# Letting expert 1's weight loads go out while the last attention pairs are still being transposed by DMA

## The chip, the cores and the metric

The kernel runs on one core of one Trainium2 chip. The metric is the device time of one execution in microseconds (us), and a version is judged by the median over several executions.

## The reference

The work is a sparse attention followed by a mixture of eight experts with balanced (Sinkhorn) gates. Shapes: q, k and v are 4 x 8 x 768 x 64 (batch, head, position, feature); the attention output becomes x of 3072 x 512.

```python
k_sum = k.reshape(B, H, nb, 32, D).max(axis=3)      # 24 blocks of 32 keys
v_sum = v.reshape(B, H, nb, 32, D).mean(axis=3)
a = softmax over [ scores within |i-j| < 16 , scores with k_sum + log(32) ]
x = concat heads of ( a @ [v, v_sum] )               # 3072 x 512
P = exp(x @ w_gate - max)
for _ in range(8):
    P /= P.sum(1, keepdims=True); P /= P.sum(0, keepdims=True); P *= N / E
out = sum over e of  P[:, e] * ( relu(x @ w1[e]) @ w2[e] )
```

## The kernel before

Heads are handled in 16 pairs, four for each of the four batch entries. Each pair needs q and k with the features on the partitions (qT, kT), v as it comes (v_x), the two edge strips of v that reach into the neighbouring tile (V_e), scores, exponentials, masks, the values product, a normalisation, and a transposition of the result into xT, the input of the experts. While the pairs run, TensorE also computes expert 0 in plain form (hps, yps). Experts 1 to 7 follow in a long stage with a Strassen-like scheme of seven products per block (pa, pb, pg, xy), which fills the time from about 128 us to the end. Between the two lies the bridge: the eight Sinkhorn rounds on the gates P_sb, spread between the last matmuls of expert 0 and the first of expert 1.

How transfers are issued in the attention part:

- GpSimd (POOL) issues every load from memory: k, q and v of each pair with a cast from 32 to 16 bits, and the expert weights `w1` and `w2`. These go through the software queue q0.
- SyncE (SP) issues, through the hardware queue q1, four small copies for V_e per pair (`near_values`, L362 and L364), for pairs 12 to 15 the transposes of k and q (`tr_dma`, L310), and for pairs 10 to 14 the transpose of the normalised result into xT (`x_dma`, L314). Earlier pairs are transposed by TensorE.
- Each of the two queues has eight completion semaphores that it uses in turn, so that a transfer is issued only when the one eight places earlier in the same queue has landed.

The order of instructions on each engine is fixed when the program is built, by a list scheduler (`Plan`). Each unit of work is entered by `add` with an engine, a planned cost, its dependences, a priority and a `lag`, the planned time after its end until its result can be used. For a DMA the cost is the issue time on the queue and the lag is the planned landing. The plan sets the order alone; the waits at run time are for the real landings.

The loads of expert 1's first weights are entered last of all on POOL: four tiles of `w1` (`load_w1(1, i)`, two DMAs of 128 KB each, L176) and one tile of `w2` (`load_w2(1)`, one DMA of 1024 KB, L187). In front of them stands a unit `hold`. It copies one element of each of the four qT buffers that pairs 12 to 15 use (L820), and so cannot end before the transposes of q of pairs 12 to 15 have landed; POOL runs in order, so the weight loads stand behind it.

Names used later: `kT12`, `qT12`, `near12`, `x10` and so on mean the DMA of that kind for that pair. `logits(b)` (L531) multiplies xT of the four pairs of batch entry b with the gate weights. `normalize` (L509, L510) writes a buffer `xs`, of which there are two; `x_dma` reads it, so the normalisation of pair i+2 cannot write before `x_dma(i)` has landed.

Of the kernel before, what the change touches and what calls it, by code (L numbers as in the profile page):

```python
# [10 lines left out]
BF16 = mybir.dt.bfloat16  # L11
# [22 lines left out]
class Plan:  # L34
# [12 lines left out]
    def add(self, eng, cost, fn, deps=(), prio=0.0, opens=(), uses=(), lag=0.0):  # L47
        u = Unit(eng, cost, fn, [d for d in deps if d is not None], prio, list(opens), lag)
        for b in list(opens) + list(uses):
            b.users.append(u)  # L50
        if uses and eng != "PE":
            u.prio -= 100.0
        self.waiting.append(u)
        return u
# [62 lines left out]
def kernel(  # L117
# [10 lines left out]
    nc = tc.nc  # L128

    B, H, S, D = q.shape  # L130
    G = S // 128
# [6 lines left out]
    NP = (B * H) // 2  # L138
    PB = H // 2
    SCALE = 1.0 / float(D) ** 0.5  # L140
    W = 16
# [4 lines left out]
    VD = D + 1  # L146
# [68 lines left out]
    NB = PB  # L215
    NE = 2
# [7 lines left out]
    attn = early.enter_context(tc.tile_pool(name="attn", bufs=1))  # L224
    aps = early.enter_context(tc.tile_pool(name="aps", bufs=1, space=PSUM))
    if True:

        ident = attn.tile([128, 128], BF16, name="ident")
        held = attn.tile([1, 1], BF16, name="held")
        band = attn.tile([128, LIVE], BF16, name="band")  # L230
        m_blk = attn.tile([128, G, 64], BF16, name="m_blk")
        qT = [attn.tile([128, W + S + W], BF16, name=f"qT{i}") for i in range(NB)]
        kT = [attn.tile([128, S], BF16, name=f"kT{i}") for i in range(NB)]
# [10 lines left out]
        add = plan.add  # L244
# [51 lines left out]
        def tr(i, z, tag):  # L296
            st = at.pop(("st", i, z))
            t = at["t", i, z] = bank(tag, "tkq", BF16)
            for g in range(G):
                if i < PB:  # L300
                    for j in range(2):
                        nc.tensor.transpose(t[64 * j:64 * j + 64, g * 128:(g + 1) * 128],
                                            st[:, j, g, :], ident)
                else:
                    nc.tensor.transpose(t[:, g * 128:(g + 1) * 128],  # L305
                                        st[:, g, :, :].rearrange("p j d -> p (j d)"), ident)

        def tr_dma(i, z):
            r, st = i % NB, at.pop(("st", i, z))
            nc.sync.dma_start_transpose(out=(kT[r][:], qT[r][:, W:W + S])[z].rearrange("c (g t) -> c g t", g=G),  # L310
                                        in_=st[:].rearrange("p g j d -> p (g j d)"))
# [45 lines left out]
        def near_values(i):  # L357

            sv, ve = v_x[i % NQ], V_e[i % NE]
            for j in range(2):  # L360
                c0, q0 = VD * j, 64 + 32 * j
                nc.sync.dma_start(out=ve[q0 + W:q0 + 2 * W, 1:G, c0:c0 + VD],  # L362
                                  in_=sv[128 - W:128, j, 0:G - 1, :])
                nc.sync.dma_start(out=ve[q0:q0 + W, 0:G - 1, c0:c0 + VD],  # L364
                                  in_=sv[0:W, j, 1:G, :])

        def scores(i, h):
            sg = at["sg", i, h] = banks2("sg")
            for s in range(HG):
                for j in range(2):  # L370
                    score_mm(i, sg[:, j, s * LIVE:(s + 1) * LIVE], j, HG * h + s, 0, LIVE)
# [244 lines left out]
        U = {}  # L616
        last = [None, None]
# [19 lines left out]
        def pair_start(i, prio):  # L637
            o = i - NB
            war_k = [U.get(("S", o, 0)), U.get(("S", o, 1)), U.get(("km", o))]
            war_q = war_k[:2] + [U.get(("ss", o, 0)), U.get(("ss", o, 1))]  # L640
            tag = "m" if i < PB else "a"
            for z in range(2 if i >= PB else 1):
                if i >= 12:
                    U["tr", i, z] = U["kT", i, z] = add("SP", 1.25, lambda z=z: tr_dma(i, z),
                                                        [U["kq"[z], i]] + (war_k, war_q)[z], prio, lag=5.0)
                    continue
                buf = Buffer(tag)
                U["tr", i, z] = add("PE", 0.4, lambda z=z: tr(i, z, tag),
                                    [U["kq"[z], i], U["ident"]] + (war_k, war_q)[z]
                                    + [U["tr", i, 0] if z else U.get(("S", i - 1, 1 if i > PB else 0))],  # L650
                                    prio, opens=[buf])
                U["kT", i, z] = add({"ACT": 0.8} if z == 0 else {"ACT": 0.8, "DVE": 0.95},
                                    0, lambda z=z: tr_out(U["kT", i, z].on, i, z), [U["tr", i, z]], prio,
                                    uses=[buf])
            if i < PB:
                query_half(i, 0, prio)
            U["km", i] = add("DVE", 0.95, lambda: key_max(i), [U["kT", i, 0]] + war_q[2:], prio)
            buf = Buffer("a")
            U["vs", i] = add("PE", 0.4, lambda: block_sums(i),
                             [U["v", i]] + ([U.get(("A", i - NE, 1))] if i >= PB else []), prio + 0.01, opens=[buf])  # L660
            U["Vs", i] = add("DVE", 0.36 if i < PB else 0.84, lambda: block_out(i), [U["vs", i]],
                             prio + 0.01, uses=[buf])
# [37 lines left out]
            return U.get((what, n % PB, n // PB)) if n >= 0 else None  # L700

        def pair_whole(i, prio):
            U["near", i] = add("SP", 2.5, lambda: near_values(i), [U["v", i], U.get(("A", i - NE, 1))], prio,
                               lag=1.9)
            for h in range(2):
                buf = Buffer("s")
                U["S", i, h] = add("PE", 0.28, lambda h=h: scores(i, h),
                                   [U["kT", i, 0], U["kT", i, 1], U.get(("ed", i - 2))], prio, opens=[buf])
                U["X", i, h] = add("ACT", 0.97, lambda h=h: score_exp(i, h), [U["S", i, h]], prio, uses=[buf])
                U["mk", i, h] = add("DVE", 0.56, lambda h=h: masks(i, h),  # L710
                                    [U["X", i, h], U.get(("A", i - 2, 1))], prio)
            U["ed", i] = add("DVE", 0.78, lambda: edges(i),
                             [U["X", i, 0], U["X", i, 1], U["mk", i, 1], U.get(("A", i - NE, 1))], prio)
            bufs = [Buffer("a"), Buffer("a")]
            U["ss", i, 0] = U["ss", i, 1] = add("PE", 0.22, lambda: summaries2(i),
                                                [U["km", i], U["kT", i, 1], U.get(("A", i - NE, 1))], prio,
                                                opens=bufs)
            for h in range(2):
                U["sx", i, h] = add("ACT", 0.46, lambda h=h: summary_exp(i, h), [U["ss", i, h]], prio,
                                    uses=[bufs[h]])  # L720
            for h in range(2):
                buf = Buffer("a")
                U["A", i, h] = add("PE", 0.4, lambda h=h: values(i, h),
                                   [U["mk", i, h], U["ed", i], U["sx", i, h], U["Vs", i], U["near", i]],
                                   prio, opens=[buf])
                U["no", i, h] = add("DVE", 0.68, lambda h=h: normalize(i, h),
                                    [U["A", i, h], U.get(("xt", i - 2))], prio, uses=[buf])
            if 10 <= i < 15:
                U["xt", i] = U["x", i] = add("SP", 1.25, lambda: x_dma(i), [U["no", i, 0], U["no", i, 1]], prio,
                                             lag=4.5)  # L730
            else:
                buf = Buffer("a")
                U["xt", i] = add("PE", 0.35, lambda: to_xT(i), [U["no", i, 0], U["no", i, 1]], prio, opens=[buf])
                U["x", i] = add({"ACT": 0.8, "DVE": 0.9}, 0, lambda: x_out(U["x", i].on, i), [U["xt", i]], prio,
                                uses=[buf])
# [55 lines left out]
        c0 = add("DVE", 3.8, constants, [], -5.0)  # L791
# [11 lines left out]
        for i in range(PB, NP):  # L803
# [3 lines left out]
            if i % PB == PB - 1:  # L807
# [7 lines left out]
                    zero.extend(U["w2d"])  # L815
                expert0(b * S, xs)
                expert0(b * S + HS, xs)
        def hold():
            for r in range(12 % NB, NB):
                nc.gpsimd.tensor_copy(out=held[0:1, 0:1], in_=qT[r][0:1, W:W + 1])  # L820

        last[0] = add("POOL", 0.3, hold, [last[0]] + [U["kT", i, 1] for i in range(12, NP)])
        for i in range(4):
            load(("w1n", i), lambda i=i: load_w1(1, i), 0.85, 1.3)
        load("w2n", lambda: load_w2(1), 0.85, 5.0)
# [13 lines left out]
    if True:  # L839
# [351 lines left out]
        for n in range(LAG, len(groups)):  # L1191
            g0, q0 = g, q
            g = group(*groups[n])
            q = pair(*groups[n - LAG])
            e, j, i = groups[n]
# [48 lines left out]
        last = [pair(*groups[len(groups) - LAG + n], spare=bool(n % 2), c1_at=c1s[n], tail=True) for n in range(LAG)]  # L1244
# [6 lines left out]
        A, B, C, D = last  # L1251
# [42 lines left out]
```

## Time and profile before

| what | us |
|---|---|
| median of 7 executions | 676.3 |
| lowest and highest of the 7 | 674.63 and 678.41 |
| the profiled execution | 674.77 |
| span of the profiled execution, first to last instruction | 673.0 |
| TensorE busy in the span | 662.7 |

The profiled execution lies near the low end of the runs; 1.8 us of it lie outside the span. Times below are counted from the start of the span. A timeline row gives start, duration, engine, line, operation and tiles, the number of instructions merged, and in brackets the idle time before it with the one that ended it. A row of the table by stretches gives the stretch and its length, the busy time (and instruction count) of PE, PEld, DVE, ACT and POOL, the granted clock, the summed share of the DMA engines' time taken by packets, and GB/s.

### The profile page before, as it was taken

The numbers are of one execution on the slowest core, as the hardware profiler recorded it, in microseconds if no ns is written. First come the engines' busy times: TensorE is split into PE (matmuls) and PEld (weight loads), VectorE is DVE, ScalarE is ACT, GpSimd is POOL, SyncE is SP. The second block draws the span as 40 slices with busy tenths as digits, with TensorE's granted clock in tenths as the row PEclk, the third lists the DMA queues.
The fourth block names the chain that finished last, engine by engine and source line by source line (L and its number), as shares of the span: only waits on it lengthen the run. The fifth ranks groups of instructions, "written<-read, shape, count | busy, mean of one in ns | idle before, by whom it ended". The sixth has DMA issues, their size and how long they took to land.

```text
span 673.0 us, 13531 instructions
## 1 busy us (share of the span) xinstructions
PE 662.7 (98%) x5111; PEld 434.4 (65%) x5111; DVE 579.7 (86%) x1433; ACT 402.3 (60%) x783; POOL 131.6 (20%) x177
## 2 busy tenths in 40 slices
PE   7999999999999999999999999999999999999996
PEld 4666655555666666666666666666666666666665
DVE  6878889777799988998899988998899889998885
ACT  4777776565777765555655565555555555556552
POOL 8699622122101010201010010101020101100001
PEclk9999999999999999999999999999999999999999
DMA  9999969000613050311422061405031142201224
GB/s 118 190 145 145 151 91 157 10 1 1 79 12 36 1 79 1 37 13 22 58 23 27 1 78 10 39 1 79 1 33 17 22 58 21 29 0 48 82 91 158
DMA packets 124018, 36.46 MB, mean 54 GB/s; under 512 B 110384, under 2 KB 121136, under 8 KB 123952
## 3 DMA queue, kind: packets, MB, share of 16 engines
q0 software_dynamic: 104672, 26.22, 42.2%
q1 hardware_dynamic: 18464, 8.83, 5.9%
q8 instruction: 40, 0.66, 0.4%
q10 hardware_dynamic: 816, 0.54, 0.3%
q14 instruction: 26, 0.21, 0.1%
HBM read 52.45 MB, written 6.29 MB: 87 GB/s over the span
## 4 chain that ended last, share of the span: by engine, by line
PE 93%; DVE 4%; DMA 1%; issue 1%; ACT 0%; POOL 0%; DVEq 0%; ACTq 0%
PE xy L913 36%; PE pg L907 16%; PE pa L907 11%; PE pb L907 11%; PE hps L200 6%; PE yps L210 6%; PE sg L334 1%; DVE hf L857 1%; DMA vx<-in_v_dram 1%; PE vs L342 1%; PE tkq L305 1%; PE av L406 1%; PE av L412 1%; PE ss L430 1%; PE tx L517 0%
## 5 line engine op out<-in xcount | busy, mean ns | idle before, releaser
L913 PEld LDWEIGHTS <-hf 128*128 128x128 f16 x2352 | 230.1, 98 | 95.6 <-issue 0.5
L913 PE MATMUL xy<-w,hf 128*128 128x256 f16 x1312 | 183.4, 273 | 0.0
L913 PE MATMUL xy<-ws,hf 128*128 128x256 f16 x984 | 147.6, 273 | 0.1
L191 ACT ACTIVATE hf<-pg 128x512 f16<-128x512 f32 x84 | 50.2, 597 | 150.9 <-PE pg L907 150.9
L1049 DVE SCALAR_TENSOR_TENSOR out_acc<-xy,P_sb,out_acc 128x512 f32<-128x512 f32 x164 | 115.0, 742 | 2.1 <-PE xy L913 2.1
L854 DVE TENSOR_TENSOR hf<-hf 128x512 f16<-128x512 f16 x252 | 100.0, 423 | 8.8
L907 PE MATMUL pa<-xT,w 128*128 128x512 f16 x336 | 99.9, 379 | 0.0
L907 PEld LDWEIGHTS <-w 128*128 128x128 f16 x672 | 65.8, 98 | 44.3 <-issue 1.1
L857 DVE TENSOR_TENSOR hf<-pb,c 128x512 f16<-128x512 f32 x84 | 58.1, 691 | 38.6 <-PE pb L907 32.4
L176 POOL DMA_DIRECT2D w<-in_moe_w_dram x56 | 41.8, 758 | 220.6 <-PE pg L907 191.9
L907 PEld LDWEIGHTS <-ws 128*128 128x128 f16 x504 | 49.3, 98 | 25.4
L941 ACT COPY c<-pg 128x512 f32<-128x512 f32 x84 | 49.2, 585 | 22.4 <-PE pg L907 22.4
L857 DVE TENSOR_TENSOR hf<-pg,c 128x512 f16<-128x512 f32 x84 | 57.1, 679 | 0.8 <-PE pg L907 0.8
L926 ACT COPY pg<-pa 128x512 f32<-128x512 f32 x84 | 47.9, 570 | 4.8
L191 ACT ACTIVATE hf<-pa 128x512 f16<-128x512 f32 x84 | 50.6, 603 | 0.0
L907 PE MATMUL pg<-xTs,w 128*128 128x512 f16 x168 | 50.0, 379 | 0.2
L907 PE MATMUL pg<-xT,w 128*128 128x512 f16 x168 | 50.0, 379 | 0.1
L907 PE MATMUL pb<-xT,ws 128*128 128x512 f16 x168 | 50.0, 379 | 0.0
L907 PE MATMUL pg<-xTs,ws 128*128 128x512 f16 x168 | 50.0, 379 | 0.0
L907 PE MATMUL pb<-xTs,ws 128*128 128x512 f16 x168 | 50.0, 379 | 0.0
L934 ACT COPY c<-pb 128x512 f32<-128x512 f32 x84 | 49.8, 593 | 0.0
L200 PE MATMUL hps<-xT,w 128*128 128x384 f16 x256 | 48.6, 326 | 0.0
(141 smaller groups left out, 818.1 us busy)
## 6 DMA issues: line engine op xcount, KB each, us to landing
w<-in_moe_w_dram POOLq DMA_DIRECT2D x8, 1024.0 KB, 8.9
w<-in_moe_w_dram POOLq DMA_DIRECT2D x56, 128.0 KB, 3.5
out_dram<-out_acc SPq DMA_DIRECT2D x20, 256.0 KB, 2.0
qst<-in_q_dram POOLq DMA_DIRECT2D x32, 96.0 KB, 5.9
vx<-in_v_dram POOLq DMA_DIRECT2D x16, 192.0 KB, 6.3
kst<-in_k_dram POOLq DMA_DIRECT2D x24, 96.0 KB, 6.3
w<-in_moe_w_dram POOLq DMA_DIRECT2D x2, 512.0 KB, 8.1
kst<-in_k_dram POOLq DMA_DIRECT2D x4, 192.0 KB, 4.7
```

Source lines behind the costliest of these rows:

```text
L176: nc.gpsimd.dma_start(out=t[:, :, h, :], in_=moe_w1[e].rearrange("(dk p) f -> p dk f", p=128)[:, :, f:f + 128])
L191: nc.scalar.activation(out=out, in_=in_, func=AF.Relu, bias=0.0, scale=1.0)
L200: nc.tensor.matmul(hp[:, 0:n], lhsT=w1s[e][:, dk, 128 * f:128 * (f + 1)], rhs=xT[:, dk, t0:t0 + n], start=(dk == 0), stop=(dk == KD - 1))
L210: nc.tensor.matmul(yp[:], lhsT=h[:, f, c * 128:(c + 1) * 128], rhs=w2s[e][:, f, :], start=(f == 0), stop=(f == KF - 1))
L854: nc.vector.tensor_tensor(out=out, in0=in0, in1=in1, op=ALU.subtract)
L857: nc.vector.tensor_tensor(out=out, in0=in0, in1=in1, op=ALU.add)
L907: nc.tensor.matmul(bank[:], lhsT=w[:, dk, :], rhs=x[:, dk, :], start=start and dk == 0, stop=dk == KH - 1, skip_group_check=True)
L913: nc.tensor.matmul(bank, lhsT=a(f)[:, 128 * c:128 * (c + 1)], rhs=w[:, f, :], start=start and f == 0, stop=f == FH - 1, skip_group_check=True)
L926: nc.scalar.copy(out=B["g"][:], in_=B["a"][:])
L934: nc.scalar.copy(out=B["c5"][:], in_=B["b"][:])
L941: nc.scalar.copy(out=B["c2"][:], in_=B["g"][:])
L1049: nc.vector.scalar_tensor_tensor(out=acc, in0=src, scalar=P_sb[:, t, e:e + 1], in1=acc, op0=ALU.mult, op1=ALU.add)
```

## The change

The unit `hold` and its one-element tile are taken out. Three planned lags are set higher. `near_values` gets a choice of issuing engine, which for pair numbers 0 to 15 always gives SyncE as before, since the other branch begins at 16.

```diff
-        held = attn.tile([1, 1], BF16, name="held")
...
-                nc.sync.dma_start(out=ve[q0 + W:q0 + 2 * W, 1:G, c0:c0 + VD],
+                eng = nc.gpsimd if i >= 16 else nc.sync
+                eng.dma_start(out=ve[q0 + W:q0 + 2 * W, 1:G, c0:c0 + VD],
...
                     U["tr", i, z] = U["kT", i, z] = add("SP", 1.25, lambda z=z: tr_dma(i, z),
-                                                        [U["kq"[z], i]] + (war_k, war_q)[z], prio, lag=5.0)
+                                                        [U["kq"[z], i]] + (war_k, war_q)[z], prio, lag=6)
...
-            U["near", i] = add("SP", 2.5, lambda: near_values(i), [U["v", i], U.get(("A", i - NE, 1))], prio,
-                               lag=1.9)
+            U["near", i] = add(*(("POOL", 3.6) if i >= 16 else ("SP", 2.5)), lambda: near_values(i),
+                               [U["v", i], U.get(("A", i - NE, 1))], prio, lag=2.2)
...
                 U["xt", i] = U["x", i] = add("SP", 1.25, lambda: x_dma(i), [U["no", i, 0], U["no", i, 1]], prio,
-                                             lag=4.5)
+                                             lag=5)
...
-        def hold():
-            for r in range(12 % NB, NB):
-                nc.gpsimd.tensor_copy(out=held[0:1, 0:1], in_=qT[r][0:1, W:W + 1])
-
-        last[0] = add("POOL", 0.3, hold, [last[0]] + [U["kT", i, 1] for i in range(12, NP)])
         for i in range(4):
             load(("w1n", i), lambda i=i: load_w1(1, i), 0.85, 1.3)
         load("w2n", lambda: load_w2(1), 0.85, 5.0)
```

In the built program the instructions of TensorE, VectorE, ScalarE and SyncE stand in the same order as before. GpSimd's are the same too but for the four one-element copies, which are gone.

More of the change, by code (lines that the diff above doesn't have):

```diff
@@ L361, in near_values @@
                 c0, q0 = VD * j, 64 + 32 * j
-                nc.sync.dma_start(out=ve[q0 + W:q0 + 2 * W, 1:G, c0:c0 + VD],
+                eng = nc.gpsimd if i >= 16 else nc.sync
+                eng.dma_start(out=ve[q0 + W:q0 + 2 * W, 1:G, c0:c0 + VD],
                                   in_=sv[128 - W:128, j, 0:G - 1, :])
-                nc.sync.dma_start(out=ve[q0:q0 + W, 0:G - 1, c0:c0 + VD],
+                eng.dma_start(out=ve[q0:q0 + W, 0:G - 1, c0:c0 + VD],
                                   in_=sv[0:W, j, 1:G, :])
```

## The prediction

> **What bounds the kernel now.** I read the page's busy times and its chain of waits first, then a table by stretches, then the timelines of POOL, SP and PE around the change.
>
> ```profile
> PE 662.7 (98%) x5111; PEld 434.4 (65%) x5111; DVE 579.7 (86%) x1433; ACT 402.3 (60%) x783; POOL 131.6 (20%) x177
> ...
> PE 93%; DVE 4%; DMA 1%; issue 1%; ACT 0%; POOL 0%; DVEq 0%; ACTq 0%
> ```
>
> TensorE is busy 662.7 of 673.0 us and carries 93% of the chain. The change takes no TensorE work out, so it can act on the time only through TensorE's idle time. The stretches show where that is (first PE, then PEld, DVE, ACT, POOL):
>
> ```profile
> 80.00:98.00 18.00, 18.00 (x183) 10.05 (x181) 15.46 (x40) 14.02 (x22) 1.94 (x6) 1.00 0.87 115
> 98.00:119.00 21.00, 21.00 (x219) 12.05 (x218) 18.69 (x53) 12.23 (x22) 6.68 (x9) 1.00 1.35 144
> 119.00:124.00 5.00, 5.00 (x53) 2.94 (x52) 1.62 (x7) 3.14 (x6) 0.06 (x1) 1.00 0.00 2
> 124.00:155.00 31.00, 30.08 (x161) 15.67 (x160) 26.43 (x70) 17.91 (x36) 6.47 (x11) 1.00 0.00 1
> ```
>
> From 80 to 124 us TensorE has no idle time at all. From 124 to 155 it has 0.9 us, of which 0.8 is a Sinkhorn matmul waiting for DVE. So there is next to nothing to gain in this profile, and every wait that the change adds is paid in full. POOL around the change:
>
> ```profile
> 79.62 1.02 POOL L274 DMA_DIRECT2D vx<-in_v_dram  x1 [2.23 <-PE av L412]
> ...
> 97.41 0.18 POOL L820 COPY held<-qT 1x1 bf16<-1x1 bf16 x1 [6.97 <-DMA qT<-qst]
> 97.86 5.94 POOL L176 DMA_DIRECT2D w<-in_moe_w_dram  x8 [0.28 <-issue]
> 103.73 0.96 POOL L187 DMA_DIRECT2D w<-in_moe_w_dram  x1
> ```
>
> POOL has nothing else to do from 80.6 us on; hold keeps the weights back until 97.9. And the first users of these weights:
>
> ```profile
> 123.11 0.35 DVE L1104 TENSOR_REDUCE rs_sb<-P_sb 128x24 f32<-128x192 f32 x1 [3.27 <-ACT P_sb L535]
> ...
> 123.71 0.23 DVE L857 TENSOR_TENSOR ws<-w 128x256 f16<-128x256 f16 x1
> ```
>
> The last load (w2) lands 14.2 us after its issue, at 117.9. DVE's weight sums stand behind the first Sinkhorn row sum, which waits until 123.1 for the last gate logits and not for weights. Earlier weights start nothing earlier.
>
> **What the skill says.** The Trainium skill, page "DMA: Bandwidth & Descriptors", three places. "Issuing engines are not separate DMA queues": DMAs started by different engines run on the same 16 DMA engines and interleave. "Queues, rings and completion order": a DMA engine takes turns between its queues packet by packet, and a completion count lands only after all earlier writes of that engine, across its queues; so a transpose's landing can be held by another queue's bytes. The trace agrees: transposes that had the engines to themselves (kT14, qT14, x10) landed 2.8 us after issue, those beside the weight loads (x11, x12, x13) 5.7, 9.2 and 10.0 us after. "Rules for kernel authors": a transpose beside ordinary DMAs needs no ordering, so hold is not there for safety; the trace, where x11 to x13 overlap the loads, agrees.
>
> **The change, part by part.**
>
> *Four copies on POOL gone*: 3 x 0.18 + 0.63 = 1.2 us, on an engine that was waiting. Worth 0. *Lags and the engine choice*: instruction order is as before on every engine but POOL; worth 0. *Weight loads earlier*: the eight w1 DMAs are issued from 80.6 us at 0.74 us each (5.94 / 8). Eight completion semaphores rotate: the eighth waits for the landing of v of pair 15 (79.62 + 6.5 = 86.1), and w2 waits for the first w1 DMA. So w2 goes out near 87 to 89 instead of 103.7, all some 15 to 17 us earlier. Gain on the path: 0, by the paragraph above. Their bytes now compete with what SP issues between 80 and 103 us. For each of those transfers: issue from SP's timeline, landing by its own time to landing, and the instruction that waits for its semaphore:
>
> | transfer | issued | landed | first wait | slack |
> |---|---|---|---|---|
> | near11 | 80.75 to 82.67 | 86.8 | PE 93.1 | 6.3 |
> | qT13 | 83.44 | 87.0 | PE 93.7 | 6.7 |
> | kT14, qT14 | 85.53, 86.90 | 88.3, 89.7 | PE 101.0 | 11.3 |
> | near12 | 88.22 to 90.13 | 92.1 | PE 100.4 | 8.3 |
> | x10 | 90.83 | 93.6 | DVE 100.75 (buffer xs) | 7.1 |
> | kT15, qT15 | 92.24, 93.62 | 96.7, 97.3 | PE 105.6 | 8.3 |
> | near13 | 94.93 to 97.36 | 99.3 | PE 105.0 | 5.7 |
> | x11 | 98.46 | 104.2 | PE 104.25 | 0.05 |
> | x12 | 103.71 | 112.9 | DVE 113.4 (buffer xs) | 0.5 |
> | x13 | 108.38 | 118.36 | DVE 118.38 (buffer xs) | 0.0 |
>
> The key row is x11. logits of batch entry 2 (L531, 24 small matmuls) need it:
>
> ```profile
> 98.46 1.78 SPq L314 DMA_TRANSPOSE xT<-xs  x1
> ...
> 103.98 0.87 PEld L531 LDWEIGHTS <-xT 128*128 128x128 f16 x24
> ```
>
> Before, x11 went out just behind the first w1 load and landed with 0.05 us to spare. After, it goes out behind nearly all the weights.
>
> *When will x11 land?* I count DMA work. A transpose: kT14 and qT14 landed 1.35 us apart with SP issuing that far apart (upper end); 192 KB at the 215 GB/s of that stretch is 0.9 (lower end); I take 1.1. A near set: 0.4, an estimate from its 41 KB. The weights: in the stage before, the engines were busy from about 99 to 118.4, 19.4 us, with x11, x12, x13 and two near sets in it: 19.4 - 3.3 - 0.8 = 15.3 us for 2 MB, losses from mixing included; at the 155 to 175 GB/s of that stage the bytes alone take about 12.6. So 12.6 to 15.3. Where does this fit in? The DMA shares between 85 and 97 us add up to 5.8 busy of 12 us:
>
> ```profile
> DMA  1899319990599502020202049960899349980092
> ```
>
> so 6.2 us are free there, and about 1.7 more from 97 to 99: 7.9 in all. At 99 us there are then 12.6 - 7.9 = 4.7 to 15.3 - 7.9 = 7.4 us of work still queued when x11 enters. If x11 waits for all of it, it lands at 99 + 4.7 + 1.1 + 0.3 = 105.1 to 107.8 (0.3 from last byte to landing, what is left of 2.8 us). The nearest rows, x12 and x13, which also entered behind w2, took 9.2 and 10.0 us: 107.7 to 108.5. I take 106.8, so TensorE waits 106.8 - 104.2 = 2.6 us at L531. Bounds: 0 if x11 takes its turns without its neighbours' backlog (2.8 to 5.7 us), 4.3 by x13's row.
>
> *What lies ahead of it.* kT14 to near13 also go from 2 to 4.5 us to some 6 to 10 us, later by 4 to 6 against slacks of 5.7 to 11.3: mostly covered, near13 and x10 just. kT15, qT15 and near13 are in the same queue ahead of x11 and needed after it, so their lateness hides behind x11's. x10 would first hold DVE at L510 (100.75), and behind that masks and edges of pair 14, needed by PE at 112.8 with DVE nearly full (9.6 of 10 us busy from 100 to 110).
>
> *What is relieved.* x12 to x14 and near14, near15 land in about 2 to 4 us instead of 4 to 10. Nothing on TensorE waited for them in this profile: 0. In executions slower than the profiled one they may have been late, since their slack is 0 to 0.5; that could be worth up to 676.3 - 674.6 = 1.7 us.
>
> Sum against the profiled execution: 674.77 + 2.6 = 677.4. The median of the runs lies 1.5 us higher, so 676.3 + 2.6 = 678.9.
>
> **The rivals.** *A, x11 late* (above): 678.9, own range 677.7 to 680.6 (stall 1.4 to 4.3). For it: slack 0.05, no idle time to absorb it, and w2 is queued 10 us earlier than x11. *B, not slower*: x11 gets through in time, since SP's queue has its own turns on each DMA engine, and the weights are done earlier than I count. It decides at x11 landing before 105.6, a stall under 1.35 us. For it: the low end of my count gives 105.1. Against: x12, in the same place before, took 9.2 us. Time 676.3 to 677.6. *C, faster*: x11 is in time and the median run loses the small waits at x12 and x13: 674.8. Against: this profile shows no such waits. *D, a longer pile-up*: SP's eight-in-flight limit delays its own issues, DVE is held at x10, near12 and near13 come late too. Each DMA at 9 to 10 us from issue: stall 5 to 6, 681.8. Against: slacks of 6 and more. *E, no effect*: the weights are held elsewhere. Only the semaphores of queue q0 could, until about 88; that still leaves w2 ahead of x11. Counted in B.
>
> **How the numbers follow.** A 0.57, D 0.15, B and E 0.17, C 0.11. So slower by over 0.2% (1.35 us, about what a measurement of this kernel can tell from no change) 0.72, within 0.17, faster 0.11. The time is A's, 678.9. The range leaves out most of C and the upper part of D: 675.4 to 682.0.
>
> **What would show it.** In the profile after: w1 issues on POOL from 80.6 and w2 near 88; x11's time to landing at 7 us or more; a PE wait for a DMA of xT at L531 near 104.3 of 1.5 to 4 us, and the same shift in everything after; x12 to x14 landing in under 5 us. I am wrong if L531 starts on time, or if PE's idle time between 80 and 124 stays near zero.

## The result, and the profile after

The median after is 681.65 us (14 executions, 679.09 to 685.48) against 676.3 (33 executions, 674.49 to 679.6): ratio 1.0078, 95% interval 1.0061 to 1.0096. The change costs 5.3 us. The profiled execution after took 683.48 us, span 681.7, so it lies above its median, as that of before lay below; between the two profiles stand 8.7 us of span.

The page's busy times and its chain by engine, after:

```profile
PE 665.4 (98%) x5111; PEld 435.3 (64%) x5111; DVE 579.8 (85%) x1433; ACT 402.5 (59%) x783; POOL 130.4 (19%) x173
...
PE 91%; DVE 3%; DMA 3%; POOL 1%; issue 1%; SPq 0%; ACT 0%; DVEq 0%; ACTq 0%
```

The same 5111 matmuls now take 2.7 us longer, and the share of DMA in the chain has grown from 1% to 3%. POOL's timeline shows that the edit does what it says:

```profile
80.10 1.02 POOL L273 DMA_DIRECT2D vx<-in_v_dram  x1 [2.23 <-PE av L412]
81.11 5.21 POOL L176 DMA_DIRECT2D w<-in_moe_w_dram  x7
86.72 0.75 POOL L176 DMA_DIRECT2D w<-in_moe_w_dram  x1 [0.40 <-issue]
88.01 0.89 POOL L187 DMA_DIRECT2D w<-in_moe_w_dram  x1 [0.55 <-DMA w<-in_moe_w_dram]
```

The w1 loads leave from 81.1 and w2 at 88.0, 15.7 us earlier than before. The table by stretches (PE first; the granted clock of TensorE, 1.00 at full speed, third from the end) shows where the time went:

```profile
80.00:98.00 18.00, 18.00 (x187) 10.12 (x186) 15.50 (x41) 13.79 (x23) 7.85 (x10) 1.00 1.77 159
98.00:104.00 6.00, 3.01 (x21) 1.54 (x19) 3.15 (x8) 1.93 (x3) 0.00 (x0) 1.00 1.38 143
104.00:119.00 15.00, 11.85 (x123) 6.55 (x124) 9.35 (x27) 6.41 (x10) 0.00 (x0) 0.77 0.61 68
119.00:135.00 16.00, 15.23 (x140) 8.91 (x139) 10.67 (x34) 8.04 (x16) 0.52 (x1) 1.00 0.13 26
```

TensorE stands idle for 3.0 us between 98 and 104 and for 3.15 between 104 and 119. PE's list of waits in this part and its timeline say for what:

```profile
PE av L412 <- DMA Ve<-vx: 6.1, 1, 6.1
```
```profile
100.66 0.35 PE L406 MATMUL av<-vx,em 128*128 128x65 bf16 x6
107.15 0.50 PE L412 MATMUL av<-Ve,Ee 128*128 128x130 bf16 x3 [6.14 <-DMA Ve<-vx]
107.44 0.54 PE L406 MATMUL av<-vx,em 128*128 128x65 bf16 x6
...
109.53 1.89 PE L210 MATMUL yps<-w,h 128*128 128x512 f16 x4
...
112.00 1.04 PE L210 MATMUL yps<-w,h 128*128 128x512 f16 x4
112.88 0.74 PE L531 MATMUL lp<-wg_bf,xT 128*128 128x8 f16 x24
```

One wait of 6.1 us, for the edge strips of pair 12 (near12). After it four yps matmuls take 1.89 us where they otherwise take 1.04. I cut the stretches finer along that change:

```profile
98.00:104.70 6.70, 3.01 (x21) 1.54 (x19) 3.15 (x8) 1.93 (x3) 0.00 (x0) 1.00 1.39 139
104.75:111.50 6.75, 4.35 (x32) 2.31 (x32) 3.19 (x11) 0.97 (x1) 0.00 (x0) 0.50 0.95 98
111.60:119.00 7.40, 7.40 (x95) 4.24 (x92) 6.06 (x17) 5.43 (x9) 0.00 (x0) 1.00 0.22 38
```

From about 104.7 to 111.5 the granted clock is 0.50. So the 8.7 us are 6.1 of wait and 2.7 more of busy time (665.4 less 662.7); all else cancels to 0.1. The 4.35 us that TensorE was busy at half clock account for about 2.2 of the 2.7, half of 4.35. The rest is as small as the scatter of this sum: the profile of e7 below has 663.6 busy with no half clock in this part. And the DMA view for what was issued from 87.7 to 98 us, with the time to landing at the end of each row:

```profile
w<-in_moe_w_dram POOLq DMA_DIRECT2D x1, 1024.0 KB, 19.3
Ve<-vx SPq DMA_DIRECT2D x4, 10.2 KB, 13.0
qT<-qst SPq DMA_TRANSPOSE x1, 13.8
xT<-xs SPq DMA_TRANSPOSE x1, 14.3
kT<-kst SPq DMA_TRANSPOSE x1, 10.7
```

near12 took 11.3 to 14.5 us instead of 1.9. The last of its four copies landed at 107.0; w2 landed at 107.3 and x10, next in SP's queue, at 107.5. SP itself fell behind too:

```profile
93.22 3.98 SPq L313 DMA_TRANSPOSE xT<-xs  x1
97.38 4.90 SPq L309 DMA_TRANSPOSE kT<-kst  x1
102.45 2.34 SPq L309 DMA_TRANSPOSE qT<-qst  x1
...
108.28 1.22 SPq L313 DMA_TRANSPOSE xT<-xs  x1
```

The issue of one transpose lasted up to 4.9 us. Before, that of kT15 took 1.2:

```profile
92.24 1.21 SPq L310 DMA_TRANSPOSE kT<-kst  x1
```

x11 (the last of the rows after) went out only at 108.3, when the weights were in, and landed 2.9 us later.

### The profile page after: what moved, and what is told of

Its sections match the earlier page's. It is cut to its first block, busy times and chain, and to the rows that moved or that the text cites. A ratio compares the mean times of both kernels' runs of the same rounds, so it can differ in the third digit from the quotient of the medians.

```text
span 681.7 us, 13522 instructions
## 1 busy us (share of the span) xinstructions
PE 665.4 (98%) x5111; PEld 435.3 (64%) x5111; DVE 579.8 (85%) x1433; ACT 402.5 (59%) x783; POOL 130.4 (19%) x173
## 4 chain that ended last, share of the span: by engine, by line
PE 91%; DVE 3%; DMA 3%; POOL 1%; issue 1%; SPq 0%; ACT 0%; DVEq 0%; ACTq 0%
PE xy L908 36%; PE pg L902 16%; PE pa L902 11%; PE pb L902 11%; PE yps L210 6%; PE hps L200 5%; DMA Ve<-vx 2%; PE sg L333 1%; DMA qst<-in_q_dram 1%; DVE hf L852 1%; PE vs L341 1%; PE tkq L304 1%; PE av L479 1%; PE av L412 1%; PE av L406 1%
```

## The experiments

All keep the order of instructions on PE, DVE, ACT and SP as it was, except for matmuls of zeros or a moved issue where that is said. The wait at L412 is for near12, the wait at the logits (L531 to L534, by how many lines the edit adds) for x11.

**e1, lags only.** The changed kernel with hold put back.

```diff
+        def hold():
...
+        last[0] = add("POOL", 0.3, hold, [last[0]] + [U["kT", i, 1] for i in range(12, NP)])
```

> The changed kernel with hold put back: the new lags stay, the weight loads wait for the transposes of q as before. Theory (the early weight loads alone cost the time): the order of instructions is that of before on every engine, so the median is that of before, ratio 0.998 to 1.002, near12 lands 1.9 us after its issue. Rival (the planned landing times have a part in it): at least 2 us slower than before.

Measured: 676.45, ratio 0.9989 (0.9969 to 1.0008). near12 lands 1.9 us after its issue again. The lags cost nothing that can be told from no change; the loss is the loads' alone. Its profiled execution also shows what the 0.05 us of slack of x11 mean in the old order, in the timeline of PE:

```profile
104.09 0.22 PE L532 MATMUL lp<-wg_bf,xT 128*128 128x8 f16 x3
105.82 0.68 PE L532 MATMUL lp<-wg_bf,xT 128*128 128x8 f16 x21 [1.51 <-DMA xT<-xs]
...
108.89 1.57 PE L210 MATMUL yps<-w,h 128*128 128x512 f16 x4
```

x11 landed 1.5 us late here, 6.8 us after issue, and the clock is at 0.50 for 3.4 us after that:

```profile
106.60:110.00 3.40, 3.40 (x31) 2.10 (x28) 2.37 (x8) 1.11 (x2) 0.00 (x0) 0.50 1.56 179
```

PE busy is 664.5, 1.8 above the profile of before. So in this execution 1.5 us of lateness cost 3.3.

**e2 and e3, one half of the weights early.** hold stands between the two: in e2 w1 goes early and w2 is held, in e3 w2 goes early and w1 is held. In outline:

```diff
 # e2                                   # e3
+for i in range(4): load(w1n, i)        +load(w2n)
+hold                                   +hold
+load(w2n)                              +for i in range(4): load(w1n, i)
```

> The eight w1 loads (1 MB) go out from 81 us, w2 (1 MB in one DMA) stays behind hold at about 98. Theory (w2's single large DMA, queued ahead of near12, makes near12 late): near12 lands about 5 to 8 us after issue, by 99, so TensorE does not wait at L412; x11 may then land after L531 wants it, by 0 to 2 us, since it enters together with w2: 676 to 678.5. Rival (any 1 MB ahead is enough): a wait at L412 for the copies into Ve of 2 us or more, 679 to 682.

> w2 goes out alone at 81 us, the eight w1 loads stay behind hold at about 98. Theory (it takes both: w2 must stand directly ahead of near12 with the w1 loads in front of it): w2 is served from 83 to 92, near12 lands 5 to 9 us after issue at 95 to 99, no wait at L412, 676 to 678. Rival (w2 alone does it): near12 lands after 101 and TensorE waits 1 us or more at L412, 679 or more.

Measured: e2 684.24, ratio 1.0111 (1.0092 to 1.0130), the slowest of all; e3 680.65, ratio 1.0060 (1.0041 to 1.0080). In both near12 lands in time, at 99.8 and 96.7, and there is no wait at L412, as the theories said. The times expected do not hold, since x11 takes its place: TensorE waits 7.8 us for it in e2 and 3.1 in e3. In e3 x11 took 5.7 us from issue, as it did before; it was late since SP, behind its slow issues, sent it out at 102.2 and not at 98.5. In e2 both came together. It went out at 102.1 and took 10.4. The hold itself ended late there (qT15 landed at 100.9), so w2 went out at 101.5, right ahead of x11. The DMA view for these:

```profile
w<-in_moe_w_dram POOLq DMA_DIRECT2D x1, 1024.0 KB, 10.6
...
xT<-xs SPq DMA_TRANSPOSE x1, 10.4
```

w2 landed at 112.1, x11 at 112.5.

**e5, hold until near12 has landed.** Two POOL copies read the strips of pair 12 in place of the copies from qT.

```diff
...
+        def hold_near():
+            for j in range(2):
+                p = slice(64 + 32 * j, 96 + 32 * j)
+                nc.gpsimd.tensor_copy(out=held[p, 0:1], in_=V_e[12 % NE][p, 1, VD * j:VD * j + 1])
+        last[0] = add("POOL", 0.3, hold_near, [last[0], U["near", 12]])
```

> The changed kernel with the weight loads held only until near12 has landed (two one-element-wide POOL copies read the strips of pair 12), about 92 us instead of 97.9 with hold and 81 without. Theory (near12 is what the early loads make late): no wait at L412; the weights now run from 92 to 113, beside kT15, qT15, near13 and x11. If the prediction's step on x11 is right, x11 lands 2 to 4 us late at L531: 678 to 680. Rival (near12 was the only tight one): 676 to 677.

Measured: 682.37, ratio 1.0082 (1.0051 to 1.0113). With near12 safe, its list of PE waits has in this part only:

```profile
PE lp L532 <- DMA xT<-xs: 8.1, 1, 8.1
```

x11 went out at 101.2, 2.1 us behind w2, and took 11.2 us; the two landed at 112.4 and 112.3. The rival, that near12 was the only tight transfer, falls; the theory's 2 to 4 us and 678 to 680 were too low as well. The wait predicted at the logits exists when near12 is in time, and in this profile it is three times the 2.6 us that I gave it. The profiled execution is the slowest of the six, 685.59 us, so 8.1 is likely more than its usual wait.

**e8, near12 from another engine's queue.**

```diff
-                eng = nc.gpsimd if i >= 16 else nc.sync
+                eng = nc.scalar if i == 12 else nc.sync
```

> The changed kernel with the four copies of near12 issued by ScalarE, so that they do not stand in SP's queue behind kT14 and qT14. Theory A (near12 is late because SP's queue serves its transposes in order and each waits its turn beside the weights): near12 lands in 4 to 8 us, no wait at L412; the next late one is x10 or kT15, 677.5 to 680. Theory B (all queues share the engines and w2 is ahead, whichever queue near12 uses): near12 still takes 10 us or more and the time stays at 681 or above.

Measured: 681.7, ratio 1.0064 (1.0038 to 1.0090). near12 took 9.2 to 10.0 us from ScalarE's queue too, though in SP's it took up to 14.5. It landed at 101.1, 3.4 us before L412 read it; TensorE had waited 2.5 us for ScalarE, which had stood at these issues, and later waited 1.9 us for x11. The landing lies between the two theories' ranges, and the time, in B's, holds a wait of the edit's own making, so it does not decide. The landings show an order, though. In five profiles weights went out ahead of near12 and it stayed in SP's queue behind qT14 (the changed kernel, e2, e3, e4 and e10); in each its first copy landed 0.2 to 0.4 us after qT14, in the changed kernel at 101.9 after 101.5. In e8 it landed from 99.1 on, and qT14 only at 105.2.

How much of near12's lateness that order makes is not shown, since its time in SP's queue varies as much. The run e4 below is the changed kernel with matmuls of zeros added only behind the issue and landing of near12, and in its profile, which has a lower clock early on (0.83 from 16 to 30 us), the four copies took 6.0 to 6.8 us:

```profile
Ve<-vx SPq DMA_DIRECT2D x4, 10.2 KB, 6.3
```

**e10, w2 in eight pieces.**

```diff
-        nc.gpsimd.dma_start(out=w2s[e][:], in_=moe_w2[e].rearrange("(fk p) d -> p fk d", p=128))
+        src = moe_w2[e].rearrange("(fk p) d -> p fk d", p=128)
+        for f in range(KF if e == 1 else 1):
+            fs = slice(f, f + 1) if e == 1 else slice(0, KF)
+            nc.gpsimd.dma_start(out=w2s[e][:, fs, :], in_=src[:, fs, :])
```

> The changed kernel with w2 loaded in eight DMAs of 128 KB instead of one of 1024 KB; same bytes, same rows. Each piece waits for the landing of the DMA eight places before it, a w1 load, so never more than eight are queued. Theory A (what is queued behind w2 lands only when w2 is done, because it is one deep DMA): near12 lands by 100 and the copies and transposes behind it too; wait at L412 gone, 676.5 to 679. Theory B (the bytes ahead count, not their packing): near12 and its neighbours land as late as in the changed kernel, 680 to 683.

Measured: 680.97, ratio 1.0064 (1.0038 to 1.0090), not to be told from the changed kernel. near12 landed by 101.0, 9.0 to 9.9 us after issue and ahead of the last piece of w2 (103.3). That does not show that the packing matters: in e4, with w2 in one DMA, near12 landed 6.6 us ahead of it (100.3 and 106.9). The time stays in theory B's range: the waits at L412 (0.2 us), behind VectorE at L513, held by x10 (1.1) and for x11 (2.2) add up to 3.5 us, and the clock falls after them.

**e4, e9 and e11, is the lower clock a cost of its own?** Matmuls of zeros where TensorE waits: in e4 22 of them (3.5 us) ahead of L412 of pair 12 in the changed kernel, in e11 the same in the kernel before, in e9 36 ahead of the logits in e5.

```diff
+            if i == 12 and h == 0:
+                for _ in range(22):
+                    nc.tensor.matmul(av[:, 0:384], lhsT=zeros[:],
+                                     rhs=zeros[:, None, :].to_broadcast([128, HG, 128]), start=False, stop=False,
+                                     skip_group_check=True)
```

> The changed kernel with 22 matmuls of zeros (384 columns, about 3.5 us at full clock) put between the two products of pair 12, where TensorE waited 6.1 us in the profile; they add zeros to the sum. Theory (beside the wait itself, the fall of the granted clock after it costs 2.7 us in the profile): the clock stays at 1.00 after 104 us, the PE busy time less the 3.5 us of fill is that of before, and the median is 1 to 2.7 us below the changed kernel's. Rival (the wait alone, with the clock a bystander): same as the changed kernel's, or slower where the wait is shorter than the fill.

> Control for e4: the kernel before with the same 22 matmuls of zeros at L412 of pair 12, where it has no wait. Theory: they cost their full 3.5 us, less what the later start gives x11 and its neighbours (0 to 1 us): 678.8 to 680. e4 measured 682.0, so the early weights would still cost it 2 to 3 us. Rival (the fill hides something else in before): 676 to 678.5.

> e5 (weights free after near12; TensorE waits 8.1 us for x11 at L531, and the stretch from 104 to 119 us then shows a granted clock of 0.66) with 36 matmuls of zeros (384 columns each, about 5.8 us at full clock) put just ahead of L531, where it waits anyway. Theory (a long wait costs its length and again a stretch at a lower clock, about 3 us here): the clock stays at 1.00, and the median is 2 to 3 us below that of e5 (682.4), at 679.4 to 680.4. Rival (the clock reading is a bystander): same as e5 within 0.5 us.

Measured: e4 682.0, ratio 1.0074 (1.0049 to 1.0100); e11 678.63, ratio 1.0037 (1.0023 to 1.0052); e9 681.11, ratio 1.0079 (1.0052 to 1.0106). As times, e4 and e9 miss what the theory expected and fit the rival's "the same" better: e4 is where the changed kernel is, and e9 and e5 have nearly the same ratio (1.0079 and 1.0082). In e4's profile there was no wait to fill, since near12 had landed at 100.3 and the fill began at 103.6. So it says nothing of the clock. In e9's, x11 landed at 109.7, some 5 us after the logits would have wanted it and 0.8 before they began; the fill took the wait's place and that bit more. What e9 does show is the clock and the busy time. The timeline of PE shows the fill, and no wait behind it:

```profile
104.63 6.01 PE L531 MATMUL lp<-zeros 128*128 128x384 bf16 x36
110.48 0.74 PE L537 MATMUL lp<-wg_bf,xT 128*128 128x8 f16 x24
```

PE is busy 668.8 us in e9, less 6.0 of fill 662.8, that of before (662.7); in e5 it was 666.3. The stretch from 104 to 119, first of e5, then of e9:

```profile
104.00:119.00 15.00, 6.93 (x69) 3.91 (x68) 5.59 (x14) 3.05 (x5) 0.00 (x0) 0.66 0.76 114
104.00:119.00 15.00, 15.00 (x136) 8.87 (x135) 8.51 (x26) 6.91 (x13) 0.00 (x0) 1.00 0.97 125
```

The clock is 0.66 in e5 and 1.00 in e9. So the 3.6 us in e5 are the idle time's second bill; 3.2 of them are half of the 6.44 us that TensorE was busy at half clock. That filling a wait saves time is not shown. e11 came out 0.2 us below its expected range: the fill costs the kernel before only 2.3 of its 3.5 us. Some of it may hide in waits of that kernel's own, as e1's; its profile does not show them.

**e6 and e7, the other way: weights later.** In e6 w2 waits for x14, in e7 w1 waits for x11 as well, in place of hold.

```diff
+        def hold_x(i):
+            t = i // PB * S
+            nc.gpsimd.tensor_copy(out=held16[0:1, 0:1], in_=xT[0:1, i % PB, t:t + 1])
...
+            if b == 2:            # in logits(b); e7 only
+                hold_x(11)
+                for i in range(4):
+                    load_w1(1, i)
+            if b == B - 1:        # e6 and e7
+                hold_x(14)
+                load_w2(1)
```

> hold as before for w1; w2 is held until x14 has landed, at about 119 us. VectorE's sums of w2 come after 150 us, so nothing waits for it. Theory (w2's large DMA is what makes x12 and x13 take 9 to 10 us, and in slower executions they hold VectorE at L510): x12 and x13 land in 3 to 6 us, median 0 to 1.7 us below before. Rival (they never cost anything): same as before within 0.1%.

> w1 is held until x11 has landed (about 101.3 us), w2 until x14 has landed (about 119). Theory: x11 lands 2.8 us after issue with nearly 3 us to spare, so executions in which it lay behind the first w1 loads lose their small wait at L531; median 0 to 2 us below before. Rival: same as before within 0.1%; or slower, if w1 landing near 113 collides with x12 and near15.

Measured: e6 675.99, ratio 0.9993 (0.9976 to 1.0009), no difference, though x12 still took 7.4 us there and only x13, with 3.9, came as early as expected; e7 675.29, ratio 0.9986 (0.9972 to 1.0000), about 1 us better, with the end of the interval at no change. In e7 the DMA view gives for x11, issued at 98.3:

```profile
xT<-xs SPq DMA_TRANSPOSE x1, 2.8
```

It lands at 101.1, 3 us before it is wanted. If the kernel before has a small loss here, x11 beside w1 is its likely place, as in e1's profile; but the intervals of e6 and e7 overlap, so this is not shown. e7 has the lowest median found.

## Why the prediction was right, and where it was not

- **Direction, range and the gain of zero.** Slower was forecast at 0.72, and 681.65 lies inside 675.4 to 682.0, near its upper end. The forecast of 678.9 is 2.7 us short of it. That the range held, by 0.35 us, is in part luck: of the signs named, the issue times and the relief came, but x11 landed 2.9 us after issue and not 7 or more, and TensorE had no wait at L531. In that profile the time was made up by a wait elsewhere and by a lower clock that was not priced.
- **No gain.** Right: the weights landed 10.6 us earlier and started nothing earlier. The relief of x12 to x14 and near14, near15 came as said (2.8 us and mostly 1.9 us from issue) and was worth 0, again as said.
- **Issue times.** w1 from 80.6, w2 near 87 to 89: 81.1 and 88.0.
- **The DMA work count.** It put the end of weights and transposes at 105.1 to 107.8; w2 landed at 107.3. near13, the last transfer ahead of x11, landed only at 110.4, so the count fits the weights and not the transfers it was meant for. Two readings in it were loose: the free time came from digits that stop at 9, where the share of the DMA engines' time can go above 1 (1.45 from 99 to 118.4 us); and x12 went out together with w2 (103.71 and 103.73), not behind it.
- **The step that failed: "What lies ahead of it".** It gave every transfer in front of x11 6 to 10 us and called near12 covered by its slack of 8.3. near12's last copy landed 14.9 us later than before, of which 2.4 are a later issue. I had counted its place as one of many shares of the backlog; it stood behind kT14 and qT14 in SP's own queue, and qT14 took 13.8 us. So in the profiled execution the wait fell at L412, from 101.0, ahead of the logits.
- **The main mechanism, x11 at the logits.** It did not happen in the profile after: SP's long issues pushed x11's own to 108.3, behind the weights. A late x11 is real nevertheless: e2, e3 and e5 each have it as the only wait, at 7.8, 3.1 and 8.1 us. The size was too small by up to three times, in two terms. The prediction let x11 go out at 99; it went out at 101.2 to 102.2 in these three. And it took 10.4 and 11.2 us in e2 and e5, landing with w2. In e9, which runs as e5 does up to the logits, it took 9.8 and landed 4.6 us ahead of w2, so landing with w2 is no rule.
- **Rival D.** Much of it is what the profile shows: near12 late, SP's issues delayed, a wait of 5 to 6 us; and its 681.8 is near the median. Its reason for the delay is not. From 85 to 112 us the transfer eight places earlier had always landed before SP's previous issue ended; the issues themselves lasted longer (3.98 and 4.90 us). I gave it 0.15 since the slacks were 6 us and more; that was the wrong reading of them.
- **The term that was missing.** No step priced what follows a wait. Of the 8.7 us, 2.2 to 2.7 are matmuls at half clock. The Trainium skill has it: page "TensorE: Matmul & The Clock Gate", section "Part 1: The HAM clock gate (the "warmup" mystery)", says that the clock is halved after an idle window of about 3.4 us and given back after a busy one. The traces agree on the size: the halved stretches last 3.4 us in e1, 6.8 after and 10.2 in e5, one, two and three times 3.4. They differ on what it takes, and there the measurement decides. In each profile with several clock changes in its course they lie whole multiples of one stretch apart: in e8 the clock falls at 13.50 and at 112.49 us, 29 times 3.41. Counted back from them, these are stretches of e8:

```profile
88.60:91.99 3.39, 2.45 (x31) 1.30 (x29) 2.71 (x8) 0.35 (x1) 0.92 (x2) 1.00 1.65 151
92.01:95.40 3.39, 1.85 (x15) 0.98 (x15) 1.01 (x2) 2.80 (x4) 0.00 (x0) 1.00 2.07 148
95.42:98.80 3.38, 3.38 (x46) 2.21 (x45) 3.19 (x11) 2.25 (x4) 0.00 (x0) 1.00 1.34 139
...
109.09:112.48 3.39, 1.67 (x46) 1.44 (x46) 2.46 (x6) 0.55 (x2) 0.00 (x0) 1.00 0.36 69
112.50:115.89 3.39, 3.39 (x19) 1.39 (x18) 2.95 (x9) 1.18 (x2) 0.00 (x0) 0.50 0.32 59
```

The wait of 2.5 us for ScalarE falls into two of them and brought no lower clock. The shorter one of 1.9 for x11 falls into one and did, as did the 1.5 us in e1 (busy 1.89 of 3.40 us). So no whole idle stretch is needed, and the length of the wait alone does not decide. Busy 1.85 us brought nothing and 1.89 did, so no threshold follows from these figures.

What stays open: which transfer is late differs between executions of one kernel (in e4's profile near12 was in time, in the changed kernel's it was not), and only one execution of each was profiled. So what makes near12 late, w2 ahead of it, SP's queue or the way w2 is packed, is not settled: its times in e2, e8 and e10, 6.5 to 10.0 us, lie within the 6.0 to 14.5 that the same load order gave in e4 and after. Only e3's 2.1 to 3.2 lie clear of it, and there w2 had landed at 92.4, just after near12's first issue, with w1 still held. The split of the median 5.3 us into wait and clock is not measured either, only that of the profiled 8.7. The mean granted clock is on record for every execution: its median is 0.9945 over the 14 of the changed kernel, and 0.997 to 0.999 over those of before in the three rounds of experiments. Of some 680 us this is 1.7 to 3.1, an estimate of the most that the lower clock can cost, since half-clock stretches cover idle time too; the rest would be waiting.

## What to carry to other kernels

A load that nothing needs yet is not free when it shares the DMA engines with transfers that have deadlines: list the slack of each of these and ask which stands behind the whole of it, in its own queue and on the engines. Where TensorE is the bound, a wait can have a second price, a stretch of matmuls at half clock; in e1's profile 1.5 us of lateness cost 3.3, while in e8's a wait of 2.5 us brought none. A hold that looks like lost time can be the better order, and holding longer, until the last tight transfer has landed, was the variant with the lowest median, ahead by 0.14%, which is at the edge of what these runs can tell.

## What was unexpected of the hardware

- Small copies of 10 KB on one queue took 11.3 to 14.5 us beside the weights on another, 1.9 alone, and 6.0 to 6.8 in another execution with the same loads; transposes went from 2.8 to 14.3 us. In e2 and e5 a transpose issued 0.6 and 2.1 us behind the 1 MB load landed 0.4 and 0.1 us after it; in e9 one issued 0.7 us behind landed 4.6 us ahead.
- A transpose's issue on SyncE lasted 3.98 and 4.90 us under this load, 1.2 without it, so the engine that issues is slowed and not the transfers alone.
- A TensorE wait of 1.5 us (e1) was followed by 3.4 us at half clock, one of 2.5 us (e8) by none.
